# Next memory from float32 products over all 128 rows of the copied result, the two blocks' values projected one after the other, and a new written-out order

## The chip, the cores and the metric

One Trainium2 chip, one NeuronCore of it. The metric is the device time of one execution in microseconds (us); the time of a kernel is the median of its runs. One execution of each kernel is also recorded by the hardware profiler, and all views of the profile come from that one execution.

## The reference

Four layers follow each other on a sequence of 2048 rows of width 512: A, B, A, B, each behind a layer norm and added to its input. A is attention with a recurrent memory, B is linear attention.

```python
def _A_ref(x, mem0, Wq, Wk, Wv, Wo, seg_len):      # 64 segments of 32 rows, 32 heads of width 128
    mem = mem0                                      # 8 rows
    for s in range(n_seg):
        xs = x[:, s * seg_len:(s + 1) * seg_len, :].copy()
        h = jnp.concatenate([mem, xs], axis=1)      # 40 rows
        q, k, v = (jnp.einsum('btd,dhe->bhte', h, W) for W in (Wq, Wk, Wv))
        scores = jnp.einsum('bhqe,bhke->bhqk', q, k) * scale
        p = _softmax(jnp.where(mask[None, None], scores, -1000000000.0), axis=-1)
        o = jnp.einsum('bhqk,bhke->bhqe', p, v)
        o = jnp.einsum('bhte,hed->btd', o, Wo)
        mem = o[:, :M, :].copy()                    # the next segment's memory
        outs.append(o[:, M:, :])

x = x + _A_ref(_layernorm(x), ...); x = x + _B_ref(_layernorm(x), ...)   # and both once more
```

What matters here: the first 8 rows of a segment's result are the memory of the next segment, so the 64 segments of an A layer form one chain: projections, scores, softmax, values, output projection, next memory. Only the 8 memory rows of each segment are on that chain. The other rows' attention, their output, the residual and the B layers hang beside it.

## The kernel before

All weights of A (Wq, Wk, Wv, Wo, 4 MB each) stay in on-chip memory. A segment's 32 columns (8 of the memory, 24 of the segment's own rows, `hT`) are the stationary operand of TensorE (PE), in four column groups of 32, and the weights stream through as moving operands of 512 columns; each group of four matmuls that runs side by side is called a group below. The last 8 rows of each segment ("left" rows) are projected four segments at a time by `left_block` and `left_values`. Heads are handled in two blocks, b = 0 and b = 1.

A segment's stages, with the names that the order uses and the lines of the profile:

- `kq0`, `kq1`: keys and queries of block 0 and 1, by `project`: 4 steps over the width, each one group per projection. In `kq0` keys and queries share the loaded stationary operand: the first part loads it (line 2186), the second reuses it through `again` (line 2074). `kq1` loads it for every group. Then each PSUM bank is copied on ScalarE (ACT, line 1954) or VectorE (DVE, line 1955) and transposed on DVE (line 2205).
- `v`: the values. One call of `project` with both blocks as its two parts: each of 4 steps does a group for block 0, which loads, and one for block 1, which reuses. Two banks are filled together and copied to `vimg` after the last step (line 1954 or 1955).
- `mem0`, `mem1` (`mem_attention`): the memory rows' attention, block by block: scores (lines 2320 and 2312), exponential on ACT (2327), spreading by a mask on DVE (2335), values (2348, "pvm": 8 matmuls of 130 columns that need both `Pm` and the block's values), reciprocal (2353), scaling (2363 on ACT or 2365 on DVE) and transpose (2355).
- `out` (`out_proj`, line 2441): the output projection, 8 pieces of 8 matmuls of 256 columns; pieces 1 to 4 need block 0, pieces 5 to 8 block 1. The sum over heads is left in two halves, in rows 0 to 63 and 64 to 127 of the bank. One half (64 rows) is copied to `outW` (line 1954), then DVE adds the other half to it and writes `y_sb` in bfloat16 (line 2452).
- `next` (`next_mem`, line 2469): 8 small bfloat16 matmuls take 32 columns of `y_sb` as stationary operand and `selm_sb` (128 x 16, ones that select the memory rows) as moving operand, which gives the 8 memory rows transposed; a copy puts them into `hT` of the next segment, whose `kq0` waits for it.
- `x` (`x_attention`, lines 2379 to 2423): the other rows' attention of the same segment, whose output runs with the next segment's `out`. `res`, `bi`, `prep`, `leftv`: residual, the B layer's work on finished tiles of 128 rows, layer norms, left rows.

The order of everything is written out by hand: `PLACE` maps (layer, segment, stage) to one number for each operation of that stage. `schedule` sorts all operations by that number; each engine issues its own in that order and waits in it. A letter behind the number puts a copy on ACT (a) or DVE (v). PSUM banks are handed out in the same order. So an operation of PE whose input isn't ready stops PE, with all that stands behind it.

Of the kernel before, what the change touches and what calls it, by code (L numbers as in the profile page):

```python
# [1828 lines left out]
def _build_kernel(nc, A_x, A_mem0, A_Wq, A_Wk, A_Wv, A_Wo, A_seg_len, B_wqkv, B_wo, out):  # L1829
# [38 lines left out]
    NW = 3  # L1868
# [283 lines left out]

    img_no = [0, 0]
    out_no = [0]
    cnt = {"m": 0}
    LASTW = 400

    def a_layer(layer):
# [772 lines left out]
```

## Time and profile before

| | |
|---|---|
| time, median of 3 runs (lowest to highest) | 1538.91 us (1537.79 to 1543.11) |
| the profiled execution: its time, its span | 1536.93 us, 1535.2 us |
| busy share of the span: PE, DVE, ACT, GpSimd (POOL) | 96%, 82%, 59%, 13% |
| mean granted TensorE clock | 0.998 |
| `next` of the first segment to that of the last, A layer 1 | 47.3 us to 737.8 us |
| the same, A layer 2 | 783.8 us to 1485.2 us |

The profile gives PE two rows: PE for matmuls and PEld for loads of the stationary operand, which run beside matmuls. A matmul of 512 columns is shown with some 380 ns, but groups follow each other at 0.216 us: matmuls are pipelined, and a short stop of PE can be hidden under the modelled end of the matmul before it. So a stop shows in the PE row with less than it costs, and in the PEld row with more.

### The profile page before, as it was taken

The page shows a single profiled execution, that of the slowest core. Times are in us where ns is not written, and L with a number is a line of the kernel's source. Part 1 is how long each engine was busy: PE and PEld are TensorE (multiplying, and loading weights), DVE is VectorE, ACT ScalarE, POOL GpSimd, SP SyncE. Part 2 cuts the span into 40 slices and gives each one's busy share as a digit, 9 for nine tenths or more (in the row PEclk, how much of TensorE's full clock was granted, in tenths as well). Part 3 has the DMA queues.
Part 4 walks back from the last instruction along what each step waited for, and adds up shares of the span by engine and source line. Part 5 has one row for each costly group of instructions (what it writes and reads, how often), then busy time and mean ns, then how long its engine had stood idle before and what let it go on. Part 6 is the DMA issues. An engine that isn't in the chain of part 4 may idle for free.

```text
span 1535.2 us, 86722 instructions
## 1 busy us (share of the span) xinstructions
PE 1468.6 (96%) x42589; PEld 765.3 (50%) x36301; DVE 1265.8 (82%) x4106; ACT 904.4 (59%) x2630; POOL 199.9 (13%) x396
## 2 busy tenths in 40 slices
PE   7899999999999999999999999999999999999988
PEld 3444554545555544554444554554555445455444
DVE  4778888888888888888887888878888888887878
ACT  2555556555555555554555667666656666666656
POOL 3011110111111011111111110111110111111010
PEclk9999999999999999999999999999999999999999
DMA  9310100100100001001310001011100011001025
GB/s 391 97 31 23 30 17 20 27 24 24 24 20 10 23 24 24 25 24 34 59 24 21 24 21 26 24 28 24 28 16 23 24 27 27 24 24 32 16 45 135
DMA packets 81624, 60.01 MB, mean 39 GB/s; under 512 B 64040, under 2 KB 74600, under 8 KB 79720
## 3 DMA queue, kind: packets, MB, share of 16 engines
q1 hardware_dynamic: 67944, 37.58, 9.3%
q0 software_dynamic: 13152, 16.75, 3.9%
q8 instruction: 308, 5.05, 1.4%
q14 instruction: 60, 0.49, 0.1%
q10 hardware_dynamic: 160, 0.14, 0.0%
HBM read 25.57 MB, written 11.67 MB: 24 GB/s over the span
## 4 chain that ended last, share of the span: by engine, by line
PE 40%; DVE 4%; DMA 3%; ACT 2%; issue 1%; DVEq 0%
PE pb L2186 15%; PE pb L2074 9%; PE pb L2441 9%; PE pb L2086 2%; DMA arena_sb<-arena_sb 1%; DMA dx_sb<-y_sb 1%; PE pb L2391 1%; PE pb L2348 1%; PE pb L2624 1%; ACT arena_sb L1954 1%; PE pb L2411 1%; PE pb L2312 1%; PE pb L2469 1%; DVE arena_sb L1955 0%; DVE arena_sb L2205 0%
## 5 line engine op out<-in xcount | busy, mean ns | idle before, releaser
L1954 ACT ACTIVATE arena_sb<-pb 128x512 bf16<-128x512 f32 (+2 forms) x949 | 477.4, 532 | 256.8 <-PE pb L2074 141.6
L2186 PE MATMUL pb<-Wk_sb,arena_sb 128*32 128x512 bf16 x4192 | 359.0, 381 | 7.3 <-DMA Wk_sb<-in_A_Wk_dram 3.6
L2441 PE MATMUL pb<-Wo_sb,arena_sb 128*32 128x256 bf16 x10368 | 324.2, 273 | 8.6 <-DVE arena_sb L2353 5.6
L2205 DVE STREAM_TRANSPOSE arena_sb<-arena_sb 128x256 f32<-128x256 f32 x640 | 257.7, 424 | 39.5 <-ACT arena_sb L1954 34.4
L2441 PEld LDWEIGHTS pb<-Wo_sb,arena_sb 128*32 128x32 bf16 x10368 | 258.2, 97 | 61.1 <-DVE arena_sb L2353 34.9
L1971 POOL DMA_DIRECT2D dx_sb<-y_sb x246 | 125.5, 514 | 1051.6 <-DVE y_sb L2452 662.2
L2186 PE MATMUL pb<-Wq_sb,arena_sb 128*32 128x512 bf16 x3088 | 254.5, 379 | 1.4 <-DMA Wv_sb<-in_A_Wv_dram 0.7
L2074 PE MATMUL pb<-Wv_sb,arena_sb 128*32 128x512 bf16 x2560 | 249.9, 378 | 0.0
L2186 PE MATMUL pb<-Wv_sb,arena_sb 128*32 128x512 bf16 x2560 | 249.8, 378 | 0.0
L2363 ACT ACTIVATE arena_sb<-pb,arena_sb 128x128 bf16<-128x128 f32 x525 | 160.8, 368 | 103.7 <-DVE arena_sb L2398 44.7
L2186 PEld LDWEIGHTS pb<-Wk_sb,arena_sb 128*32 128x32 bf16 x4192 | 111.4, 97 | 218.5 <-issue 111.4
L2074 PE MATMUL pb<-Wq_sb,arena_sb 128*32 128x512 bf16 x2032 | 198.5, 379 | 0.8 <-issue 0.8
L1955 DVE CAST arena_sb<-pb 128x512 bf16<-128x512 f32 (+2 forms) x315 | 157.8, 504 | 46.7 <-PE pb L2074 16.9
L2365 DVE TENSOR_TENSOR arena_sb<-pb,arena_sb 128x384 bf16<-128x384 f32 (+2 forms) x392 | 159.6, 408 | 9.9
L1954 ACT ACTIVATE outW_sb<-pb 64x256 f32<-64x256 f32 x150 | 56.9, 379 | 157.6 <-PE pb L2441 120.5
L2186 PEld LDWEIGHTS pb<-Wq_sb,arena_sb 128*32 128x32 bf16 x3088 | 83.0, 97 | 96.9 <-issue 35.9
L2379 DVE TENSOR_TENSOR arena_sb<-arena_sb,wx_sb 128x640 bf16<-128x640 bf16 x256 | 115.9, 471 | 0.9
L2186 PEld LDWEIGHTS pb<-Wv_sb,arena_sb 128*32 128x32 bf16 x2560 | 68.6, 96 | 89.3 <-issue 51.6
L2401 DVE STREAM_TRANSPOSE arena_sb<-arena_sb 128x192 f32<-128x192 f32 x256 | 92.7, 362 | 22.2 <-ACT arena_sb L2363 19.8
L2452 DVE TENSOR_TENSOR y_sb<-pb,outW_sb 64x256 bf16<-64x256 f32 x162 | 68.7, 424 | 47.7 <-ACT outW_sb L1954 45.1
L2391 PE MATMUL pb<-arena_sb 128*32 128x130 bf16 x3072 | 93.4, 220 | 0.8 <-DVE arena_sb L2379 0.4
L2074 PE MATMUL pb<-Wk_sb,arena_sb 128*32 128x512 bf16 x928 | 91.6, 379 | 0.0
(128 smaller groups left out, 1784.2 us busy)
## 6 DMA issues: line engine op xcount, KB each, us to landing
Wk_sb<-in_A_Wk_dram SPq DMA_DIRECT2D x1, 4096.0 KB, 14.7
Wq_sb<-in_A_Wq_dram SPq DMA_DIRECT2D x1, 4096.0 KB, 24.0
Wv_sb<-in_A_Wv_dram SPq DMA_DIRECT2D x1, 4096.0 KB, 33.4
Wo_sb<-in_A_Wo_dram SPq DMA_DIRECT2D x8, 512.0 KB, 23.2
xs_scratch<-x_sb POOLq DMA_DIRECT2D x32, 128.0 KB, 2.0
pq_scratch<-arena_sb POOLq DMA_DIRECT2D x27, 128.0 KB, 2.3
x_sb<-xs_scratch POOLq DMA_DIRECT2D x16, 128.0 KB, 2.7
dx_sb<-y_sb SPq DMA_DIRECT2D x126, 12.0 KB
```

The source lines that it names most:

```text
L1954: return e.activation(o() if callable(o) else o, i() if callable(i) else i, ACTF.Copy)
L1955: return e.tensor_copy(o() if callable(o) else o, i() if callable(i) else i)
L1971: add(eng, lambda e: e.dma_start(o, i), 0.55 if eng == "pool" else 0.66, reads=reads, writes=writes, dsem="%s%d" % (kind, k), lat=lat + (0 ...
L2074: return pe.add_instruction(mybir.InstMatmult(name=nc.get_next_instruction_name(), engine=mybir.EngineType.PE, ins=[pe.lower_ap(x), pe.low ...
L2186: r = pe.matmul(o, blk[:, c, :], w, start=(c == 0), stop=(c == 3), tile_position=(0, 32 * j))
L2205: add("dve", lambda v: v.transpose(dst, src(img[:, k, :].bitcast(F32))), 0.445, reads=[("img", k, h) for h in range(2)], writes=[dkey])
L2363: x = e.activation(o[:, u, :], i()[:, u, :], ACTF.Copy, scale=r[:, u:u + 1])
L2365: return e.tensor_tensor(o, i(), r.unsqueeze(2).to_broadcast([128, n, 128]), ALU.mult)
L2379: add("dve", lambda v, b=b: v.tensor_tensor(Px[:, b, :].rearrange("p (n j x) -> p n j x", n=20, j=4), PQ[:, r2, b, 64:224].rearrange("p (n ...
L2391: r = pe.matmul(pv.f32()[32 * i:32 * i + 32, 130 * k:130 * k + 130], cols(b, k, i), vimg[:, r2, 4 * b + i, :], start=True, stop=True, skip ...
L2401: add("dve", lambda v, b=b, k0=k0: v.transpose(oTb[:, s1, b, :, :, k0:k0 + 3].rearrange("p h j k q e -> p k (h j) (q e)").bitcast(F32), ox ...
L2441: r = pe.matmul(tl.f32()[32 * j:32 * j + 32, 0:256], oT[:, b, f, n, :, :, e], Wo_sb[:, 16 * b + 4 * n + 2 * f + e, 256 * d:256 * d + 256], ...
```

## The change

1. `out_proj` copies all 128 rows of the bank to `outW` for a segment's result, in place of 64. `next_mem` takes its stationary operand from `outW` in float32; `selm_sb` is float32 and has ones in both halves, so that the product itself adds them. DVE still adds the halves into `y_sb`, but for the residual only; `next` doesn't wait for it.
2. The values of block 0 are projected with all 4 steps, then those of block 1. Each call loads the stationary operand itself, so there are 16 loads more in each segment. Each block's values have a resource of their own.
3. The result of the left rows goes through the same two `outW` slots in turn with the segments' results.
4. Two more selections of GpSimd in the setup fill the second half of `selm_sb`; the arena is 20 elements smaller.
5. Nearly all of the 1538 rows of `PLACE` hold new numbers.

```diff
-    selm_sb = sb("selm_sb", [128, 16])
+    selm_sb = sb("selm_sb", [128, 16], F32)
...
+        P.count += 200 + j
+        sel(scr_sb[q, 8 * d:8 * d + 8], ALU.not_equal, 1.0, 0, [[-1, 8]], 1, *SCR)
+        P.count -= 201 + j
         if j < 2:
-            sel(scr_sb[q, 8 * d:8 * d + 8], ALU.not_equal, 1.0, 0, [[-1, 8]], 1, *SCR)
+            P.count += 1
...
-            add("pe", pvm, 0.112, reads=[("Pm", k), ("v", r2, b), ("vl", g2, b)], tiles=[pv])
+            add("pe", pvm, 0.112, reads=[("Pm", k), ("v", r2, b, 0), ("v", r2, b, 1), ("vl", g2, b)], tiles=[pv])
...
         def out_proj(oT, keys, urgent, end=False):
-            w = NW - 1
+            w = out_no[0] % (NW - 1)
+            out_no[0] += 1
             if urgent:
-                w = out_no[0] % w
-                out_no[0] += 1
+                wl[0] = w
...
-            k = int(w == NW - 1)
+            k = int(not urgent)
             a, c = (slice(0, 64), slice(64, 128))[::-1 if urgent else 1]
-            v = w if urgent else 0
-            nd = evac(outW[c, v, :], lambda: tl.f32()[c, 0:256], 256, tiles=[tl], writes=[("outW", w)])
+            v = w
+            cc = slice(0, 128) if urgent else c
+            nd = evac(outW[cc, v, :], lambda: tl.f32()[cc, 0:256], 256, tiles=[tl], writes=[("outW", w)])
...
         def next_mem(s):
...
-                        r = pe.matmul(tl.f32()[32 * j:32 * j + 32, 16 * h:16 * h + 16], y_sb[:, 0, o:o + 32],
+                        r = pe.matmul(tl.f32()[32 * j:32 * j + 32, 16 * h:16 * h + 16], outW[:, w, o:o + 32],
                                       selm_sb[:, :], start=True, stop=True, tile_position=(0, 32 * j))
-                add("pe", mm, 0.04, reads=[("y", 0), "selm", "y0", "yl"], tiles=[tl])
+                add("pe", mm, 0.06, reads=[("outW", w), "selm"], tiles=[tl])
...
-            for b, tl in enumerate(project(blk, bk, (Wv_sb, "Wv", 0, False), (Wv_sb, "Wv", 1, False), fresh=(FRESH[layer] + g) // 4)):
-                evac(vimg[:, r2, 4 * b:4 * b + 4, 0:128], lambda tl=tl: tl.f32()[:, :].rearrange("p (i d) -> p i d", i=4), 512, tiles=[tl],
-                     writes=[("v", r2, b)])
+            for n, (b, lo, hi) in enumerate(((0, 0, 512), (1, 0, 512))):
+                tl = project(blk, bk, (Wv_sb, "Wv", b, False, lo, hi))[0]
+                evac(vimg[:, r2, 4 * b + lo // 128:4 * b + hi // 128, 0:128],
+                     lambda tl=tl, h=hi - lo: tl.f32()[:, 0:h].rearrange("p (i d) -> p i d", d=128), hi - lo, tiles=[tl],
+                     writes=[("v", r2, b, i) for i in range(lo // 256, hi // 256)])
```

Of `PLACE`, three rows of segment 33 of the first layer. `v` has 4 numbers of PE and 2 of copies before, and twice 4 of PE and 1 of a copy after; in `mem0` and `mem1` the first two numbers are the scores and the sixth is the values' product.

```diff
-    (0, 33, 'v'): '3471 3475 3479 3483 3491a 3497a',
+    (0, 33, 'v'): '3605 3608 3611 3613 3622a 3615 3618 3620 3623 3633a',
-    (0, 33, 'mem0'): '3474 3478 3488 3486 3492 3498 3503 3506v 3512',
+    (0, 33, 'mem0'): '3603 3604 3610 3653 3628 3632 3635 3637v 3639',
-    (0, 33, 'mem1'): '3489 3490 3496 3505 3499 3507 3513 3515v 3517',
+    (0, 33, 'mem1'): '3625 3626 3631 3642 3634 3638 3640 3644v 3647',
```

More of the change, by code (lines that the diff above doesn't have):

```diff
@@ L1876, in _build_kernel @@
     st_sb = sb("st_sb", [128, 2, 16], F32)
-    ARENA_N = 35328
+    ARENA_N = 35308
     arena = sb("arena_sb", [128, ARENA_N])
@@ L1912, in _build_kernel @@
     Px = av(2 * 640).rearrange("p (b x) -> p b x", b=2)
-    Rc = av(16, F32)
     omem = av(2 * 128).rearrange("p (r x) -> p r x", r=2)
@@ L1929, in _build_kernel @@
     za = av(128, F32)
-    za4 = av(8, F32)[:, 0:4]
     e_sb = av(D)
@@ L1933, in _build_kernel @@
     xv = av(2 * D)
+    Rc = av(10, F32)
+    za4 = av(4, F32)
     xlnT = xv[:, 0:D].rearrange("p (c x) -> p c x", c=4)
@@ L2154, in _build_kernel @@
     out_no = [0]
+    wl = [0]
     cnt = {"m": 0}
@@ L2172, in mm @@
                 def mm(pe, c=c):
-                    for i, (tl, (W, key, b, across)) in enumerate(zip(tls, parts)):
+                    for i, (tl, (W, key, b, across, *lo)) in enumerate(zip(tls, parts)):
+                        lo, hi = lo if lo else (0, 512)
                         for j in range(4):
-                            o = tl.f32()[32 * j:32 * j + 32, 0:512]
+                            o = tl.f32()[32 * j:32 * j + 32, 0:hi - lo]
                             if across:
@@ L2181, in mm @@
                                 n = (8 * j + 4 * b) * DH
-                                w = W[:, c, n:n + 512]
+                                w = W[:, c, n + lo:n + hi]
                             if i and 4 * c + j >= fresh:
@@ L2394, in pvx @@
                         return r
-                    add("pe", pvx, 0.0565, reads=[("Px", b), ("v", r2, b)], tiles=[pv])
+                    add("pe", pvx, 0.0565, reads=[("Px", b), ("v", r2, b, 0), ("v", r2, b, 1)], tiles=[pv])
                 pvv = lambda pv=pv: pv.f32()[:, 0:390].rearrange("p (k x) -> p k x", k=3)
@@ L2414, in pvl @@
                     return r
-                add("pe", pvl, 0.113, reads=[("Px", b), ("v", r2, b), ("vl", g2, b)], tiles=[pv])
+                add("pe", pvl, 0.113, reads=[("Px", b), ("v", r2, b, 0), ("v", r2, b, 1), ("vl", g2, b)], tiles=[pv])
             pvv = lambda pv=pv: pv.f32()[:, 0:260].rearrange("p (b x) -> p b x", b=2)
@@ L2462, in next_mem @@
             at(s, "next")
+            w = wl[0]
             G1, g1 = divmod(s + 1, 4)
@@ L2544, in a_layer @@
         for r in range(2):
-            add("pool", lambda p, r=r: p.memset(vimg[:, r, :, 128:130], 1.0), 0.3, writes=[("v", r, b) for b in range(2)] + ["pool"])
+            add("pool", lambda p, r=r: p.memset(vimg[:, r, :, 128:130], 1.0), 0.3, writes=[("v", r, b, i) for b in range(2) for i in range(2)] + ["pool"])
             add("pool", lambda p, r=r: p.memset(vleft[:, r, :, :, 128:130].rearrange("p b g x -> p (b g) x"), 1.0), 0.3, writes=[("vl", r, b) for b in range(2)] + ["pool"])
@@ L2633, in late_queries @@
                  (flat(oTl[:, 0].rearrange("p b h j k q e -> p (b h j k q e)")), [("oTl", 0, 0), ("oTl", 0, 1)]),
-                 (flat(vimg[:, 0].rearrange("p n x -> p (n x)")[:, 0:1024]), [("v", 0, 0), ("v", 0, 1)]),
+                 (flat(vimg[:, 0].rearrange("p n x -> p (n x)")[:, 0:1024]), [("v", 0, b, i) for b in range(2) for i in range(2)]),
                  (flat(kT.rearrange("p h j x e -> p (h j x e)")), [("kT", 0), ("kT", 1)]),
-                 (flat(vimg[:, 1].rearrange("p n x -> p (n x)")[:, 0:1024]), [("v", 1, 0), ("v", 1, 1)])]
+                 (flat(vimg[:, 1].rearrange("p n x -> p (n x)")[:, 0:1024]), [("v", 1, b, i) for b in range(2) for i in range(2)])]
         late_t = LATE[0]
```

3066 rows, old and new, of the table PLACE are left out of this document.

## The prediction

> **What bounds the kernel now.** I read the page first (engines, clock), then the busy times by stage, then the waits, then the timeline of one segment.
>
> ```profile
> PE 1468.6 (96%) x42589; PEld 765.3 (50%) x36301; DVE 1265.8 (82%) x4106; ACT 904.4 (59%) x2630; POOL 199.9 (13%) x396
> PEclk9999999999999999999999999999999999999999
> ```
>
> PE is the busiest by far and its clock is granted nearly in full, so only less PE work or fewer stops of PE shorten the time. By stage (start-up, segments of the first A layer, the B layer between, segments of the second, the end):
>
> ```profile
> 0.00:47.30 47.30, 37.95 (x733) 16.13 (x641) 23.96 (x65) 14.41 (x41) 13.19 (x40) 0.96 0.90 365
> 47.30:745.50 698.20, 667.64 (x19684) 350.49 (x16724) 586.20 (x1945) 395.35 (x1162) 90.08 (x171) 1.00 0.11 25
> 745.50:783.80 38.30, 33.77 (x884) 16.96 (x793) 32.35 (x88) 21.46 (x53) 8.28 (x16) 1.00 0.35 65
> 783.80:1492.90 709.10, 694.88 (x20368) 360.50 (x17220) 589.63 (x1942) 446.89 (x1324) 87.28 (x167) 1.00 0.10 24
> 1492.90:1535.20 42.30, 34.33 (x944) 21.22 (x936) 33.61 (x70) 26.34 (x50) 1.06 (x2) 0.96 0.60 135
> ```
>
> The first numbers are the length and PE's busy time. The segments take 698.2 + 709.1 = 1407.3 us; PE idles there for 30.6 + 14.2 = 44.8 us. That is a lower bound, since modelled ends of matmuls cover short stops. The waits name the links, each in two rows, PE's own (too little) and the load queue's (too much):
>
> ```profile
> PE pb L2348 <- ACT arena_sb L1954: 8.8, 20, 0.7
> PE pb L2441 <- DVE arena_sb L2353: 5.6, 18, 0.6
> PE pb L2469 <- DVE y_sb L2452: 5.5, 15, 0.9
> PE pb L2348 <- DVE arena_sb L2335: 3.7, 10, 0.9
> PE pb L2320 <- DVE arena_sb L2205: 3.6, 7, 1.2
> PEld pb L2320 <- DVE arena_sb L2205: 47.6, 118, 1.9
> PEld pb L2441 <- DVE arena_sb L2353: 34.9, 90, 0.8
> PEld pb L2348 <- ACT arena_sb L1954: 31.6, 87, 0.8
> PEld pb L2186 <- DVE arena_sb L1955: 25.4, 69, 0.9
> PEld pb L2469 <- DVE y_sb L2452: 23.7, 48, 1.2
> PEld pb L2348 <- DVE arena_sb L2335: 22.6, 72, 0.8
> ```
>
> Between the two I counted the real stops from the starts in the timeline: a group's start less the start of the group before it, less that shape's undisturbed pitch (0.216 us for 512 columns, 0.109 for 256, 0.056 for 130). In the segments they sum to 94 us: `out` 18.9 (most of it for block 0), the values' product of `mem0` ("pvm0") 16.5, `next` 15.5, `kq0` 11.1, pvm1 9.3, `mem1`'s scores 7.0, small ones. Each lies between its rows. These 94 us are what a shorter chain or a better order can work on.
>
> **1. The sum leaves the chain.** Segment 33 of the first layer, around `next`:
>
> ```profile
> 415.51 0.38 ACT L1954 ACTIVATE outW_sb<-pb 64x256 f32<-64x256 f32 x1 [0.26 <-PE pb L2391]
> 415.92 0.43 DVE L2452 TENSOR_TENSOR y_sb<-pb,outW_sb 64x256 bf16<-64x256 f32 x1 [0.51 <-ACT outW_sb L1954]
> 416.40 0.22 PE L2469 MATMUL pb<-selm_sb,y_sb 128*32 128x16 bf16 x8
> 416.46 0.39 PE L2624 MATMUL pb<-arena_sb 128*32 128x512 bf16 x4
> 416.70 0.19 DVE L1955 CAST arena_sb<-pb 128x32 bf16<-128x32 f32 x1
> 416.95 0.40 PE L2186 MATMUL pb<-Wk_sb,arena_sb 128*32 128x512 bf16 x4
> ```
>
> The copy ends at 415.89, the sum at 416.35, `next` starts at 416.40. With the sum's own distance of 0.05 behind the copy instead, `next` could start 0.46 earlier. From the start of `out`'s last group to `next` it is 1.216 us wherever `next` stops PE, so 0.76 after. The copy of 128 rows costs what 64 rows do; the nearest shape of 128 rows says 8 ns more:
>
> ```profile
> L1954 ACT ACTIVATE outW_sb<-pb 64x256 f32<-64x256 f32 x150 | 56.9, 379 | 157.6 <-PE pb L2441 120.5 <-PE pb L2391 35.4
> L1954 ACT ACTIVATE arena_sb<-pb 128x256 bf16<-128x256 f32 x232 | 80.9, 387 | 19.1 <-PE pb L2186 16.2 <-DVE arena_sb L1955 1.0 <-PE pb L2320 0.6
> ```
>
> But the new order uses this up in part. Adding up the PE pieces that `PLACE` puts between `out`'s last piece and `next`, at the pitches above, the mean cover over segments 1 to 61 of both layers falls from 0.96 to 0.63 us. A stop is the latency less the last group's own 0.109 less the cover; over all these segments that makes 27.3 us before and 15.5 after. It overstates (15.5 were counted before, as the pieces between come late too), so I take the ratio, 0.57: `next` gains 7 us.
>
> **2. Values in turn.** The same segment, at its attention for the memory rows:
>
> ```profile
> 411.26 0.39 PE L2074 MATMUL pb<-Wv_sb,arena_sb 128*32 128x512 bf16 x4
> 411.69 0.60 ACT L1954 ACTIVATE arena_sb<-pb 128x512 bf16<-128x512 f32 x1
> 412.29 0.60 ACT L1954 ACTIVATE arena_sb<-pb 128x512 bf16<-128x512 f32 x1
> 412.35 0.30 PE L2348 MATMUL pb<-arena_sb 128*32 128x130 bf16 x8 [0.56 <-ACT arena_sb L1954]
> 413.52 1.93 PE L2441 MATMUL pb<-Wo_sb,arena_sb 128*32 128x256 bf16 x64 [0.28 <-DVE arena_sb L2353]
> ```
>
> Both blocks' values end at once, and pvm0 waits for block 0's copy, 1.07 us from the last group's start. Only 0.13 us of PE work (`mem1`'s scores) lies between; PE stops, for 0.56 us by its row and 0.72 by the starts (1.07 less 0.22 and 0.13). After, block 1's four groups (0.86) stand in between as well. Over all segments the cover rises from 0.85 to 1.33, and the computed stop of pvm0, by the later of values and `Pm`, falls from 18.5 to 1.4. By the numbers of `PLACE` the work queued on DVE ahead of `Pm`'s mask grows from 0.23 to 0.38 us, so I take 13 of the 16.5 counted, not 15. pvm1: 18.2 to 12.6 computed, so 3 of 9.3.
>
> **3. The rest of the order.** `kq0` starts 0.52 us after `next`'s last group (0.55 after its first, 416.40 to 416.95); cover 0.57 to 0.84 us, computed stops 12.9 to 6.0: 6 of 11.1. `out` starts 1.10 after pvm0's last group (1.17 after its first, 412.35 to 413.52); computed (pieces 1 and 5) 34.8 to 29.2: 3 of 18.9. `mem1`'s scores lose: cover behind `kq1` 1.92 to 1.75, computed 1.6 to 6.4: I charge 4. Sum of 1 to 3: 7 + 13 + 3 + 6 + 3 - 4 = 28 us gained.
>
> **4. The products in float32.** The nearest row has the same shape, in the middle of the B layer:
>
> ```profile
> 759.34 0.26 PE L2750 MATMUL pb<-sel_sb,arena_sb 128*32 128x16 f32 x8
> 759.42 0.61 PE L2624 MATMUL pb<-arena_sb 128*32 128x512 bf16 x8
> ```
>
> Four products are eight records here, two rounds of four, and take 84 ns until the next group (52 and 32 by the starts). `next` has 8 products: 168 ns, against 63 now (416.40 to 416.46). That is 105 ns more, 126 times: 13.2 us of PE work, on the chain too. Bounds: 16 records at the 7 ns that lie between neighbours make 112 ns, 6 us in all; four rounds at 52 make 18 us. I take 13, the row's own.
>
> The Trainium skill (FP8 and Floating Point Precision, TensorE Precision Notes) counts four passes for true float32. By that, as an estimate, 8 products cost four times 63 ns, 24 us more in all, and the forecast below would be 1535. The row shows two rounds, not four.
>
> **5. More loads of the stationary operand.** 16 in each of 128 segments, 2048. `kq1` shows their price, as all its groups load, and `v`, where every other one does:
>
> ```profile
> 1001.39 0.39 PE L2186 MATMUL pb<-Wq_sb,arena_sb 128*32 128x512 bf16 x4
> 1001.39 0.11 PEld L2186 LDWEIGHTS pb<-Wk_sb,arena_sb 128*32 128x32 bf16 x4
> 1001.61 0.39 PE L2186 MATMUL pb<-Wk_sb,arena_sb 128*32 128x512 bf16 x4
> 1001.82 0.39 PE L2186 MATMUL pb<-Wv_sb,arena_sb 128*32 128x512 bf16 x4
> 1002.04 0.39 PE L2074 MATMUL pb<-Wv_sb,arena_sb 128*32 128x512 bf16 x4
> ```
>
> The next load runs beside a matmul and the pitch is 0.216 either way: nothing. The cover is a group of 512 columns ahead; without it a load of four costs its 0.11 us.
>
> **6. Free edits.** Two rows price them:
>
> ```profile
> POOL dx_sb L1971 <- DVE y_sb L2452: 662.2, 75, 41.7
> ```
>
> ```profile
> L2013 POOL TENSOR_SCALAR_AFFINE_SELECT arena_sb<-arena_sb 32x8 bf16<-32x8 bf16 x2 | 0.4, 185 | 0.3
> ```
>
> The sum for the residual stays on DVE (82% busy) with nobody on the chain behind it. If it comes late, the residual's DMAs on POOL's and SP's queues do; POOL has waited up to 41.7 us for it and idles 87% of the span. The left rows' slot of `outW` was last read a good segment before it is written again. The setup's two selections take POOL 0.2 us each in a stage of 47.3 us of which it works 13.2, and `selm_sb` is first used at its end. Start and end of the kernel: 0, with +-2 for their new order.
>
> **Sum.** The profiled execution took 1536.9 us: less 28, plus 13.2, is 1522.1. The median of the runs is 2.0 above it, so I forecast 1524.
>
> **Rivals.**
> *The scores become the wait (slower).* Behind `kq0` and `kq1` the cover falls by 0.13 and 0.17 us, 122 times each: 36 us. If all of it becomes stops, in place of the 4 charged, 1522 - 4 + 36 = 1554, median 1556. For it: the load queue waits there already (47.6 us, 118 times), and copies and transposes queue on two busy engines. Against: PE itself waited 3.6 us, 7 times. The kernel is slower by more than 0.3% from stops of 0.19 us a segment on (15 + 4 + 4.6 = 23 us over the 122).
> *The stops only move (no change).* PE leaves one stop and meets the next, since every segment still has the whole chain to run. If only pvm0's 13 us are won, they pay the float32 products: 1537, median 1539. For it: 94 us are left in an order that was written for this chain. Against: each latency is a constant, and the cover grew at pvm0 and `kq0` while it shrank at `next` by less than 0.46.
> *The loads are exposed (slower).* 512 more groups of loads at 0.11 us, 56 us: 1578, median 1580. Against it stands the pitch of `kq1`. The Trainium skill (TensorE: Matmul & The Clock Gate, Part 3) says a load overlaps running matmuls only when its row group differs, and here all groups use the same rows; by that rule this rival would hold, but the trace disagrees, 0.216 us a group with the load inside.
> *More is won.* If `next`, pvm0, pvm1 and `kq0` stop no longer, 52 us, less 13, and 3 at `out`: 1495, median 1497.
>
> **How the numbers follow.** Forecast 0.65, more 0.08, stops move 0.11, scores 0.13, loads 0.02, other 0.01. No change means within 0.3%, 4.6 us (1534.3 to 1543.5), about the spread of the three runs. Forecast and "more" lie below: faster 0.73; same 0.11; slower 0.16. The likeliest case's own range is 1510 to 1534: 6 to 18 us for the products and 18 to 35 for the stops. The range reaches from 1505, into "more", to 1545, over the case that nothing changes and a small part of the scores' (0.02); outside remain 0.06 below and some 0.13 above.
>
> **What the profile after would show.** The sum: `next` (line 2469's successor, float32) starts 0.06 us behind the copy into `outW`, its wait names that copy, and DVE's line 2452 is waited for by DMAs alone. Values: PE's wait for ACT's line 1954 before the values' product (8.8 us, 20 times) nearly gone. Float32: 2016 records for `next` in place of 1008 and 0.17 us until the next group. Loads: 4608 of Wv's 5120 matmuls for A on the loading line in place of 2560, the groups still 0.216 apart. Both segment stages 5 to 9 us shorter. Wrong would be: the waits of the scores for transposes (line 2320's) growing beyond some 15 us in PE's own row, a stop of PE behind each `next`, or loads that lie between matmuls and not beside them.

## The result, and the profile after

The changed kernel takes 1514.32 us (median; 1513.45 to 1517.18) against 1539.47 us for the kernel before (the median of four runs now), a ratio of 0.9837 with a 95% interval from 0.9814 to 0.9859. The forecast was 1524 (1505 to 1545), faster. The profiled execution took 1513.92 us, its span is 1512.0 us, 23.2 us less than before.

The page's engine row and clock row, and the busy times by the same stages (start-up, segments, B layer, segments, end):

```profile
PE 1458.4 (96%) x43597; PEld 835.8 (55%) x39357; DVE 1227.5 (81%) x4035; ACT 934.3 (62%) x2686; POOL 199.5 (13%) x398
PEclk9999999999999999999999999999999999999999
```

```profile
0.00:47.10 47.10, 37.90 (x727) 16.01 (x648) 24.06 (x65) 12.31 (x35) 13.61 (x42) 0.96 0.90 367
47.10:731.50 684.40, 661.37 (x20112) 386.42 (x18164) 562.67 (x1896) 416.36 (x1210) 89.13 (x171) 1.00 0.11 26
731.50:772.40 40.90, 37.22 (x960) 18.72 (x888) 33.12 (x90) 23.69 (x59) 8.70 (x17) 0.96 0.33 65
772.40:1467.60 695.20, 685.95 (x20796) 393.30 (x18648) 573.59 (x1914) 453.17 (x1328) 86.97 (x167) 1.00 0.11 24
1467.60:1512.00 44.40, 35.91 (x1028) 21.35 (x1020) 34.08 (x73) 28.79 (x57) 1.06 (x2) 1.00 0.57 139
```

The two segment stages are 13.8 and 13.9 us shorter, where 5 to 9 each were forecast. The B layer between and the end are 2.6 and 2.1 us longer; PE is busy there for 3.4 and 1.6 us more than before, so a part of what the segment stages lost is work that the new order put elsewhere. PE's share is 96% as before, although 1.5% of the time is gone, and it issues 4064 instructions more: 2048 loads for the values and 2016 for `next` (1008 products and 1008 loads). A busy share says little here; the waits do:

```profile
PE pb L2476 <- issue: 4.5, 3, 1.6
PE pb L2353 <- DVE arena_sb L2340: 4.3, 10, 0.7
PE pb L2353 <- ACT arena_sb L1954: 2.7, 7, 0.6
PE pb L2325 <- DVE arena_sb L2210: 1.8, 3, 1.3
PE pb L2446 <- DVE arena_sb L2358: 1.3, 4, 0.5
PE pb L2476 <- ACT outW_sb L1954: 1.2, 6, 0.2
PE pb L2633 <- DMA arena_sb<-arena_sb: 0.3, 1, 0.3
```

L2476 is `next`, L2353 the values' product of the memory rows, L2325 the scores, L2446 the output projection, L2633 the B layer's projections. The product's wait for a copy of the values fell from 8.8 to 2.7 us, while its wait for the mask (line 2340, before 2335) is 4.3 us after 3.7. `next`'s wait for what it reads fell from 5.5 to 1.2 us (1.4 with the copies that DVE makes), the output projection's wait for the reciprocal from 5.6 to 1.3. New are three stops of `next`, 4.5 us, for which no wait is shown (last section).

Segment 33 of the first layer again, first around `next`, then at the memory rows' attention:

```profile
408.67 0.39 ACT L1954 ACTIVATE outW_sb<-pb 128x256 f32<-128x256 f32 x1 [1.10 <-PE pb L2396]
409.11 0.32 PE L2476 MATMUL pb<-selm_sb,outW_sb 128*32 128x16 f32 x16
409.25 0.40 PE L2633 MATMUL pb<-arena_sb 128*32 128x512 bf16 x4
409.38 0.43 DVE L2458 TENSOR_TENSOR y_sb<-pb,outW_sb 64x256 bf16<-64x256 f32 x1
```

```profile
404.59 0.58 ACT L1954 ACTIVATE arena_sb<-pb 128x512 bf16<-128x512 f32 x1
405.22 0.39 PE L2077 MATMUL pb<-Wv_sb,arena_sb 128*32 128x512 bf16 x4
405.43 0.29 PE L2353 MATMUL pb<-arena_sb 128*32 128x130 bf16 x8
406.03 0.30 PE L2353 MATMUL pb<-arena_sb 128*32 128x130 bf16 x8 [0.31 <-ACT arena_sb L1954]
406.69 1.93 PE L2446 MATMUL pb<-Wo_sb,arena_sb 128*32 128x256 bf16 x64 [0.36 <-ACT arena_sb L2336]
```

The copy ends at 409.06 and `next` starts at 409.11, ahead of VectorE's sum. Block 0's values are copied at 404.59 while PE still works, and pvm0 (405.43) follows without a stop; pvm1 (406.03) still waits for its own copy.

How the 23 us come about, counted as in the prediction from starts of groups, but from the first `next` to the last and with every PE operation. "Work" is the number of records times their undisturbed pitch, and work plus stops is the length of that stretch. How records are put into groups shifts a row by up to some 2 us, but not the totals:

| us | before | after | difference | forecast |
|---|---|---|---|---|
| work | 1319.2 | 1329.4 | +10.2 | +13 |
| stops, all | 118.7 | 85.6 | -33.1 | -28 |
| of these: values' product, both blocks | 28.8 | 20.0 | -8.8 | -16 |
| `out` | 22.6 | 19.1 | -3.5 | -3 |
| `next` | 18.1 | 13.4 | -4.7 | -7 |
| projections of A, behind `next` above all | 15.9 | 6.7 | -9.2 | -6 |
| scores (line 2325, before 2320) | 7.4 | 5.2 | -2.2 | +4 |
| the B layer's projections | 7.3 | 1.5 | -5.8 | 0 |

### The profile page after: what moved, and what is told of

Read it like the earlier page. It is cut to its first block, busy times and chain, and to the rows that moved or that the text cites. A ratio compares the mean times of both kernels' runs of the same rounds, so it can differ in the third digit from the quotient of the medians.

```text
span 1512.0 us, 90803 instructions
## 1 busy us (share of the span) xinstructions
PE 1458.4 (96%) x43597; PEld 835.8 (55%) x39357; DVE 1227.5 (81%) x4035; ACT 934.3 (62%) x2686; POOL 199.5 (13%) x398
## 4 chain that ended last, share of the span: by engine, by line
PE 81%; DVE 8%; DMA 5%; ACT 3%; issue 1%; SPq 1%; POOL 0%; DVEq 0%
PE pb L2191 36%; PE pb L2446 18%; PE pb L2077 13%; PE pb L2089 3%; PE pb L2396 2%; PE pb L2633 2%; DMA dx_sb<-y_sb 2%; PE pb L2353 2%; PE pb L2416 2%; ACT arena_sb L1954 2%; PE pb L2317 1%; PE pb L2476 1%; DVE arena_sb L2210 1%; DVE arena_sb L1955 1%; DMA Wk_sb<-in_A_Wk_dram 1%
## 5 line engine op out<-in xcount | busy, mean ns | idle before, releaser
L1954 ACT ACTIVATE arena_sb<-pb 128x512 bf16<-128x512 f32 (+3 forms) x1021 | 512.0, 529 | 285.7 <-PE pb L2077 125.5
L2191 PE MATMUL pb<-Wv_sb,arena_sb 128*32 128x512 bf16 x4608 | 340.1, 379 | 1.2 <-ACT arena_sb L1954 0.9
L2446 PE MATMUL pb<-Wo_sb,arena_sb 128*32 128x256 bf16 x10368 | 328.2, 273 | 5.7 <-issue 1.3
L2446 PEld LDWEIGHTS pb<-Wo_sb,arena_sb 128*32 128x32 bf16 x10368 | 261.5, 97 | 43.5 <-DVE arena_sb L2360 16.7
L2191 PE MATMUL pb<-Wq_sb,arena_sb 128*32 128x512 bf16 x3088 | 257.5, 379 | 1.3 <-DVE arena_sb L1955 1.1
L2191 PEld LDWEIGHTS pb<-Wk_sb,arena_sb 128*32 128x32 bf16 x4192 | 118.7, 97 | 184.9 <-issue 95.4
L2368 ACT ACTIVATE arena_sb<-pb,arena_sb 128x128 bf16<-128x128 f32 x536 | 166.8, 368 | 71.3 <-DVE arena_sb L2403 27.6
L2077 PE MATMUL pb<-Wq_sb,arena_sb 128*32 128x512 bf16 x2032 | 203.1, 381 | 0.0
L2191 PEld LDWEIGHTS pb<-Wv_sb,arena_sb 128*32 128x32 bf16 x4608 | 120.9, 96 | 94.5 <-issue 13.0
L1955 DVE CAST arena_sb<-pb 128x512 bf16<-128x512 f32 (+2 forms) x239 | 117.8, 495 | 48.3 <-PE pb L2077 33.2
L1954 ACT ACTIVATE outW_sb<-pb 128x256 f32<-128x256 f32 (+1 forms) x156 | 59.7, 383 | 140.9 <-PE pb L2446 112.9
L2396 PE MATMUL pb<-arena_sb 128*32 128x130 bf16 x3072 | 105.9, 220 | 1.4 <-issue 1.2
L2406 DVE STREAM_TRANSPOSE arena_sb<-arena_sb 128x192 f32<-128x192 f32 x256 | 93.2, 364 | 15.2 <-ACT arena_sb L2368 13.3
L2396 PEld LDWEIGHTS pb<-arena_sb 128*32 128x32 bf16 x3072 | 68.4, 96 | 30.7 <-issue 7.8
## 6 DMA issues: line engine op xcount, KB each, us to landing
Wo_sb<-in_A_Wo_dram SPq DMA_DIRECT2D x8, 512.0 KB, 23.2
```

Of the source, the lines that this page charges most:

```text
L1954: return e.activation(o() if callable(o) else o, i() if callable(i) else i, ACTF.Copy)
L1955: return e.tensor_copy(o() if callable(o) else o, i() if callable(i) else i)
L2077: return pe.add_instruction(mybir.InstMatmult(name=nc.get_next_instruction_name(), engine=mybir.EngineType.PE, ins=[pe.lower_ap(x), pe.low ...
L2191: r = pe.matmul(o, blk[:, c, :], w, start=(c == 0), stop=(c == 3), tile_position=(0, 32 * j))
L2368: x = e.activation(o[:, u, :], i()[:, u, :], ACTF.Copy, scale=r[:, u:u + 1])
L2396: r = pe.matmul(pv.f32()[32 * i:32 * i + 32, 130 * k:130 * k + 130], cols(b, k, i), vimg[:, r2, 4 * b + i, :], start=True, stop=True, skip ...
```

## Experiments

The ratios are to the kernel before, run beside each run on the same chip: 1534.31 us there for e1 to e4, 1536.72 for e5 to e8, 1536.94 for e9 to e12. The stops are counted as in the table:

| run | ratio, 95% interval | work | stops | values' product | `next` | projections | scores | `out` |
|---|---|---|---|---|---|---|---|---|
| e1_old_all | 1.0181 (1.0153 to 1.0210) | 1329.7 | 131.8 | 30.4 | 4.1 | 21.3 | 17.0 | 26.0 |
| e2_old_sum | 1.0015 (0.9999 to 1.0031) | 1329.7 | 110.4 | 29.1 | 4.4 | 24.6 | 4.8 | 22.8 |
| e3_old_values | 1.0146 (1.0120 to 1.0171) | 1319.2 | 140.5 | 29.0 | 17.7 | 14.6 | 17.5 | 25.5 |
| e4_old_loads | 1.0005 (0.9990 to 1.0019) | 1319.2 | 118.5 | 29.6 | 17.4 | 16.7 | 6.3 | 22.2 |
| e5_new_wait | 1.0128 (1.0105 to 1.0151) | 1329.4 | 131.7 | 19.4 | 68.6 | 4.3 | 2.0 | 18.7 |
| e6_new_inter | 1.0101 (1.0080 to 1.0122) | 1329.5 | 126.5 | 54.9 | 12.7 | 10.8 | 6.4 | 18.4 |
| e7_new_bf16 | 0.9803 (0.9780 to 0.9827) | 1319.0 | 89.5 | 20.6 | 9.0 | 9.2 | 4.1 | 20.9 |
| e8_new_order | 1.0424 (1.0403 to 1.0445) | 1329.4 | 173.3 | 55.7 | 67.5 | 6.7 | 4.9 | 20.1 |
| e9_old_values_stay | 0.9981 (0.9968 to 0.9994) | 1319.2 | 111.8 | 24.1 | 18.0 | 13.5 | 4.6 | 23.8 |
| e10_old_sum_bf16 | 0.9963 (0.9951 to 0.9976) | 1319.2 | 115.0 | 28.6 | 5.3 | 25.3 | 4.8 | 23.3 |
| e11_changed_again | 0.9835 (0.9822 to 0.9849) | 1329.4 | 81.4 | 20.5 | 12.2 | 4.8 | 3.9 | 18.6 |
| e12_new_bf16_again | 0.9780 (0.9764 to 0.9796) | 1319.0 | 84.2 | 20.4 | 9.0 | 9.6 | 3.1 | 19.1 |

### Both edits in the order of before

```diff
+# PLACE of before; each 'v' row p0 p1 p2 p3 e0 e1 becomes
+# p0 p0+.2 p1 p1+.2 (copy: p2+.3)  p2 p2+.2 p3 p3+.2 (copy: e1)
```

> Both edits (next memory from the copied result in float32, values in turn) in the order of before, whose numbers stay; the values' eight groups stand at the old four places, block 0 at the first two. Theory (each edit takes stops from its own link): next's stops fall by some 11 us, pvm0's by 14, and the float32 products, measured at 147 against 64 ns in the profile after, cost 10.5 us: 1524 us, 0.990 of before. Rival (the stops only move in an order written for the old chain, and the new order is what won 25 us): 1539 to 1545 us. If this one reaches 1516 or less, the new order itself brings nothing.

1562.42 us, 1.8% slower: far above the theory, and above the rival (1539 to 1545) too. `next`'s stops did fall, from 18.1 to 4.1 us, but the scores' grew from 7.4 to 17.0, and the values' product gained nothing.

### The first edit alone

```diff
+# PLACE of before; values projected jointly, as before; next_mem and out_proj as changed
```

> Only the first edit in the order of before: next memory from all 128 rows of the copy in float32, without VectorE's sum on the chain; values projected jointly as before. Theory: next stops 11 us less, the products cost 10.5 us more: 1539 us, no change within 0.3%; next's wait for the sum is gone from the profile and its stops are some 4 us. Rival (a chain 0.4 us shorter in each of 126 segments shortens every segment, as the chain bounds it): 126 times 0.38 is 48 us, 1491 us. Rival (stops move on): 1545 us.

1537.45 us, no change, as the theory had it, and in its time against both rivals. The theory had not counted all of it: the stops of `next` fell by 13.7 us, not 11, but 8.7 of them moved on to the projections behind it, as the second rival has it in kind; the work grew by 10.5. The chain doesn't bound every segment, or 48 us would have gone.

### The second edit alone

```diff
+            for b in range(2):
+                tl = project(blk, bk, (Wv_sb, "Wv", b, False))[0]
+                evac(...)                      # numbers as in the first run
```

> Only the second edit in the order of before: the two blocks' values in turn, each step loading its stationary operand. Theory: pvm0's stops fall from 16 us to some 2, nothing else changes: 1525 us, 0.991. Rival (stops move on to the output projection): 1536 to 1540 us with line 2441's stops larger by as much. Rival (loads are exposed): above 1560 us.

1557.87 us, 1.5% slower: the theory fails. The output projection's stops grew by 2.9 us alone, so the first rival isn't it; in time the run is where the second, exposed loads, would put it (1.0146 is 1562 of 1539 us), and the two runs below refute that one. The values' product stops as long as before (29.0 us), but for its mask and not for the copy, and the scores stop for their transposes:

```profile
PE pb L2353 <- DVE arena_sb L2340: 14.2, 29, 1.0
PE pb L2325 <- DVE arena_sb L2210: 9.5, 20, 1.2
```

Its segment 33, with the same two operations of the kernel before beneath (scores, exponential):

```profile
414.06 1.57 ACT L1959 ACTIVATE arena_sb<-pb 128x512 bf16<-128x512 f32 x3 [0.20 <-PE pb L2191]
414.73 0.27 PE L2317 MATMUL pb<-arena_sb 128*32 128x40 bf16 x16
416.14 0.33 ACT L2332 ACTIVATE arena_sb<-pb 128x64 bf16<-128x64 f32 x2
416.75 0.30 PE L2353 MATMUL pb<-arena_sb 128*32 128x130 bf16 x8 [0.75 <-DVE arena_sb L2340]
```

```profile
410.52 0.27 PE L2312 MATMUL pb<-arena_sb 128*32 128x40 bf16 x16
411.44 0.21 ACT L2327 ACTIVATE arena_sb<-pb 128x64 bf16<-128x64 f32 x1
```

ScalarE does three copies in one go until 415.63, then small operations of the layer norm and of the other rows' attention, and only then the exponential: 1.41 us behind the scores in place of 0.92. The run had moved block 0's copy forward in ScalarE's queue, so the copy's place was the suspect.

### The same with the copies where they were

```diff
+# each 'v' row becomes p0 p0+.2 p1 p1+.2 (copy: e0)  p2 p2+.2 p3 p3+.2 (copy: e1)
```

> Values in turn in the order of before, like the run of that edit alone, but the two copies keep their old places and engines; there block 0's copy had been moved ahead of other copies of ScalarE. Theory (the place of the copy in ScalarE's queue decides: moved ahead, it held up the keys' and queries' copies, and the stops went to the scores, 7 to 17 us): the scores' stops are back at 7 us, the values' product gains a part of its 16 us, some 5: 1530 us, 0.997 of before. Rival (block 1 entering two steps later is what hurts): 1550 us or more again, with the scores' stops above 15 us.

1533.29 us, 0.9981. Only the place of one copy differs from the run above, and the 1.5% are gone: the scores' stops are at 4.6 us, those of the values' product at 24.1 in place of 28.8. Its wait for the mask is down too, from 14.2 us:

```profile
PE pb L2353 <- DVE arena_sb L2340: 6.1, 15, 0.9
```

The suspicion is shown for the second edit, and the rival falls. The run of both edits carried the same moved copy, so it tells of both together no more than that; both with the copies in place wasn't tried. If the two single runs add, it would be no change, 1.0015 times 0.9981.

### The loads alone

```diff
-            ... (Wv_sb, "Wv", 1, False), fresh=(FRESH[layer] + g) // 4)):
+            ... (Wv_sb, "Wv", 1, False), fresh=16)):
```

> Before with one number changed: every group of the values' projection loads its stationary operand (2048 loads more), nothing else. Theory (a load of four runs beside a group of 512 columns): 1539 us, within 0.3%, and the groups stay 0.216 us apart. Rival (loads are exposed where all groups use the same rows): 512 times 0.11 us, 1595 us.

1535.52 against 1534.31 us, 1.0005 (0.9990 to 1.0019). The 2048 loads cost at most 3 us by that interval, where the rival has 56. Its groups of instructions show them on the loading line, 4608 matmuls where the kernel before has 2560:

```profile
L2186 PE MATMUL pb<-Wv_sb,arena_sb 128*32 128x512 bf16 x4608 | 314.8, 379 | 0.3 <-ACT arena_sb L1954 0.3
```

### The new order with the wait put back

```diff
-                add("pe", mm, 0.06, reads=[("outW", w), "selm"], tiles=[tl])
+                add("pe", mm, 0.06, reads=[("outW", w), "selm", ("y", 0)], tiles=[tl])
```

> The changed kernel with one wait put back: next waits for VectorE's sum too, and the sum is issued ahead of next; everything else, the float32 products too, stays. Theory (the new order has used up the 0.46 us that the sum took: the cover between the output projection and next is 0.63 us in place of 0.96): the computed stops of next grow from 15.5 to 64 us, by 0.57 to 0.75 of that some 28 to 37 us: 1543 to 1551 us. Rival (the new order alone brought the gain, and next's wait was covered anyway): 1514 to 1519 us.

VectorE's sum is also issued ahead of `next` here. 1556.67 us, 3.0% above the changed kernel (1.0128 / 0.9835), 45 us. The theory's direction holds; its size (28 to 37 us) was too small, and the computed stops without the scaling (49 us more) were nearer. PE's own row:

```profile
PE pb L2479 <- DVE y_sb L2461: 45.2, 109, 1.1
```

So the sum's 0.46 us cost 13.7 us of stops of `next` in the old order and 55 us in the new one, which has 0.33 us less work between `out` and `next`.

### The new order with the values' blocks by turns

```diff
+# 'v': the same eight numbers, given to block 0 and 1 by turns; block 0's copy behind its last group
```

> The changed kernel with the eight groups of the values' projection in the old sequence, the blocks by turns, at the same eight places in the order (except in 4 of 128 segments where the PSUM banks would not suffice); block 0's copy goes behind its last group. Theory: the cover between block 0's values and pvm0 is lost, its computed stops grow from 1.4 to 26 us, 22 us by the ratio counted before: 1536 us. Rival (values in turn matter little, since pvm0 waits for its mask in any case): 1514 to 1520 us.

1553.52 us, 2.7% above the changed kernel, 41 us and not 22. The values' product alone grew from 20.0 to 54.9 us of stops, nearly all of it at block 0 (4.7 to 39.3). The load queue waits both for the mask and for the copy, where it had 28.2 and 16.5 us in the changed kernel:

```profile
PEld pb L2358 <- DVE arena_sb L2345: 43.0, 83, 1.2
PEld pb L2358 <- ACT arena_sb L1959: 38.1, 65, 1.1
```

Block 0's copy stands later in its engine's queue here, as it must. How much of the 41 us is the values' own time and how much comes from that place, by way of the mask, no run separates.

### The new order without both

The two edits above at once.

> The new order with both edits undone as far as waits go: next waits for VectorE's sum as well (sum issued ahead of it), and the values' groups go by turns as in the run with only that. Theory (links are separate and add): 32 plus 22 us on the changed kernel, 1568 us, so the new order without the edits is slower than the old order by 2%. Rival (order alone): 1514 to 1525 us. Rival (one stop covers the other, as a late next gives the values more time): 1550 us.

1603.28 us, 4.2% slower than the kernel before. The losses add (45 + 41 = 86 us; 1.0424 / 0.9835 is 6.0% above the changed kernel, 91 us), so the links are nearly separate; their stops add too (46 and 41 us more than in the changed kernel, 88 here). The theory had that and half the size, since both of its terms were too small. The new order by itself is no gain at all: it is written for the shorter links and pays where they are missing. The 4.2% are not the order's alone, as the float32 products, 10 us of work or 0.7%, are still in this run.

### Products in bfloat16

```diff
-    selm_sb = sb("selm_sb", [128, 16], F32)
-    outW = sb("outW_sb", [128, NW - 1, 256], F32)
+    selm_sb = sb("selm_sb", [128, 16])
+    outW = sb("outW_sb", [128, NW - 1, 256])
```

In the new order, and the same in the order of before with the joint values:

> The changed kernel with the copy of the result and the selecting matrix in bfloat16, so that next runs 8 bfloat16 products over all 128 rows, still without VectorE's sum; the halves are rounded before they are added. Theory (the float32 products are work on the bounding engine and on the chain): 126 times 83 ns, 10.5 us less: 1504 us. Rival (the products stand where TensorE would stop for the chain anyway, behind next for kq0): 1511 to 1514 us.

> Next memory from all 128 rows of the copy in bfloat16, without VectorE's sum on the chain, in the order of before, values jointly; the halves are rounded before they are added. Theory (without the sum the chain alone takes 14 us of next's stops off and gives 9 back at the projections; the float32 products' 10.5 us ate the rest): 1526 to 1530 us, 0.994 of before. Rival (stops go on moving: what the products no longer take, the projections' stops do): 1535 us, no change.

1508.51 us in the new order (0.9803, where the changed kernel is at 0.9837), between the theory's 1504 and the rival's 1511 to 1514. In the old one it is 1530.7 us (0.9963, where float32 gave 1.0015): less gain than the theory's 0.994, and more than the rival's none. By these ratios the new order gains 5 us from them (0.0034 of 1539). Both versions beside each other on one chip:

> The changed kernel itself, on the chip of the runs beside it, to compare with: 0.984 of before, 1510 to 1514 us.

> The version with bfloat16 copy and products in the new order once more, beside the changed kernel on the same chip. Theory (10.5 us less work on the bounding engine, a third of it lost to stops that the products had covered): 0.980 of before, 4 to 7 us below the changed kernel. Rival (no gain): equal to the changed kernel within 2 us.

1503.00 against 1512.09 us, 9.1 us less, where 4 to 7 were expected; the intervals of the two ratios lie apart. Work fell by 10.4 us, stops grew by 2.8. This version is faster than both kernels, but it rounds the two halves before they are added. The row of `next`, below that of the changed kernel, shows half the records at nearly the same time for one:

```profile
L2476 PE MATMUL pb<-selm_sb,outW_sb 128*32 128x16 f32 x2016 | 40.2, 186 | 6.4 <-issue 4.5 <-ACT outW_sb L1954 1.2 <-DVE outW_sb L1955 0.2
L2476 PE MATMUL pb<-selm_sb,outW_sb 128*32 128x16 bf16 x1008 | 27.5, 175 | 2.2 <-ACT outW_sb L1954 1.6 <-DVE outW_sb L1955 0.2
```

## Why the prediction was right

**The sum leaves the chain: shown.** From `out`'s last group to `next` it is 0.76 us in most segments in which `next` stops PE, as forecast. The copy of 128 rows takes 384 ns (387 were taken). `next` gained 4.7 us where 7 were forecast; the three stops without a wait, 4.5 us, are in its 13.4. That the freed time was spent by the order and not left lying is what the wait put back shows: 45 us.

**Values in turn: right in kind, half the size, and not for block 1.** By the table's count pvm0's stops fell from 18.3 to 4.7 us (13 less were forecast), but pvm1's rose from 10.5 to 15.2 where 3 were to be won. The computed stops of pvm1 were 12.6, and the ratio of counted to computed stops (0.5) was carried over from the old order. That ratio is what failed. Why it held only there is not shown: that other stops ahead of pvm1 had hidden half of its own in the old order is a guess, and in the run by turns pvm1 stops for 15.5 us although pvm0 again stops for 39.3. The same scaling made the two expectations of 28 to 37 and 22 us too small. For `next` the computed stops hold nearly unscaled (49 us more computed, 55 counted); for pvm0 even the unscaled 25 fall short of the 35 counted.

**The rest of the order: underrated.** The projections behind `next` gained 9.2 us (6 forecast), and the scores lost nothing: their stops fell by 2.2 (by 0.6 together with their second line, 2317, before 2312) where 4 were charged, although their cover shrank. The B layer's projections, 5.8 us, weren't in the sum: they waited for a transposing DMA, 7 times before and once after:

```profile
PE pb L2624 <- DMA arena_sb<-arena_sb: 5.8, 7, 1.3
```

I had looked at the chain's links only. In the repetition this wait is 1.2 us, with bfloat16 products 3.1, so its size is not the same in every execution of the new order, and no run shows what sets it.

**Float32: right, somewhat too dear.** `next` takes 147 ns until the next group, 52 for the first round of four and 32 for each other, against 64: 10.5 us in 126 products, where two rounds at 52 were taken (13.2). The four passes of the Trainium skill (FP8 and Floating Point Precision, TensorE Precision Notes) are not what the rows show: two records for each product, and 147 ns, not four times 64. Whether a record holds more than one pass they don't tell.

**Loads: shown to cost nothing measurable**, 1.0005, with all groups on the same rows. The rule on row groups in the Trainium skill (TensorE: Matmul & The Clock Gate, Part 3) doesn't hold for these column groups. By the rival's price 56 us were at stake, and the interval ends at 1.0019, 3 us.

**The rivals.** The scores didn't become the wait with the written order, but they did, by another way than the rival's, as soon as a copy stood in ScalarE's queue ahead of its time (17 us of stops). That the stops only move is true of the first edit in the old order (13.7 off `next`, 8.7 on to the projections), and untrue of the whole. In sum: stops 5 us better and products 3 us cheaper than forecast make the 8 us between forecast and profile. That the stops came so near is in part luck: the values' product fell short by 7 us and `next` by 2, and the projections, the scores and the B layer gave 3, 6 and 6 more than forecast.

## What to carry to other kernels

On an engine that is busy 96% of the time and is still stopped by a chain, compare for each link its latency, which hardly varied in these traces (1.22 us before and 0.76 after for `next`), with the work that the order puts into it. The difference is an estimate of the stop; here the count was from 0.5 times to 1.5 times what was computed for the larger ones. A link that gets shorter pays only where work is moved out of it. So an edit and its order are one change: the order without the two shorter links cost 4.2% (the dearer products included), the values in turn alone brought 0.2%, the product without the sum alone nothing measurable, all together 1.6%. When one operation is made ready earlier, leave its consumer's queue alone until you know what stands behind it there: one copy moved forward in a FIFO cost 1.6% by itself.

## What the runs showed of the hardware that was not expected

PE stops inside an operation, and the profile shows nothing that it waits for. In the profile after, around one of these stops:

```profile
363.71 0.31 PE L2476 MATMUL pb<-selm_sb,outW_sb 128*32 128x16 f32 x15
365.59 0.20 PE L2476 MATMUL pb<-selm_sb,outW_sb 128*32 128x16 f32 x1 [1.56 <-issue]
365.59 0.43 PE L2633 MATMUL pb<-arena_sb 128*32 128x512 bf16 x4
```

Of the 16 records of `next`, 15 start from 363.71 on, and the last not until 365.59, after a stop that PE's row gives as 1.56 us. Such stops of over 0.3 us number 9 in the changed kernel (7.2 us in all, 4.5 of them in `next`), 7 in its repetition (4.9 us), 7 and 5 in the two runs with bfloat16 products (4.3 and 2.7 us), and one in the segments of the kernel before (0.8 us). The three of `next` come at the 16th, 11th and 3rd record of the product in both executions of the changed kernel, at nearly the same times. And each of these executions' 16 stops ends 2.2 to 2.9 us after the start of a packet on the DMA queue that the profile calls instruction, while these packets start some 3.9 us apart in the median. Both point to the supply of instructions; no run varies it, so that PE runs out of them where many short ones stand together is not shown.

A float32 product with a stationary operand of 32 columns and 16 columns to move is two records, and a round of four follows the last at 32 ns where bfloat16's second round takes 25.
